# Passes that run there and back, two units' weights kept at each turn, and a DMA that adds the sums

## The chip, the core and the metric

The kernel runs on one core of a Trainium2 chip. The metric is the device time of one execution in microseconds (us). Every row below comes from one profiled execution of the kernel before; PE is TensorE, DVE VectorE, ACT ScalarE, POOL GpSimd, SP SyncE, whose queue issues nearly all transfers.

## The reference

```python
def reference(**kw):
    attn = _attn_ref(q, k, v)                 # 4 x 8 heads, 576 x 64: (scale * q k^T * decay mask) v
    x = attn.transpose(0, 2, 1, 3).reshape(2304, 512)
    h = np.maximum(x @ moe_w_in, 0.0)         # 512 -> 2048
    x = (h * h) @ moe_w_out                   # 2048 -> 512
    a, b = x @ moe2_w_a, x @ moe2_w_b         # 512 -> 1536 each
    return (a * b) @ moe2_w_out               # 1536 -> 512
```

The inputs of the MLPs come in float64 and are converted on the chip. All products need fp32 accuracy: each operand is split into a high and a low part of type fp32r, and each product is three matmuls (high by high, low by high, high by low).

## The kernel before, in words

**Stages.** The attention and four chunks of the first MLP (chunks 0 to 3 of 16, each 128 hidden columns) run first, over blocks of 512 tokens; their down sums go through `tmp` to `y1` in DRAM. Then `rest` does what is left in six **passes** of 768 tokens, two halves `j` of N2 = 384 columns each: phase 1 (`ph` 1) is chunks 4 to 15 of the first MLP, three passes; phase 2 is the twelve chunk pairs (a, b) of the second MLP, three passes.

**Units.** A pass is a list of units: six in phase 1 (two chunks each), twelve in phase 2. A unit is 2 x 2 blocks of products done with seven products instead of eight (`group`, banks 4 to 7 of PSUM): 42 matmuls of 384 columns. Its weights are two **pieces**, of 1024 and 768 columns, that were combined and stored in DRAM beforehand (`kept`). `piece(u)` loads both and splits them (`fetch`, `split`: an ACT CAST for the high part, a DVE subtraction for the low one, line 247 through the helper). There is room for the pieces of two units; unit u + 2 is loaded when unit u is done.

**Downs.** A finished hidden block goes down into banks 0 to 3, interleaved with the next units' products. A plain chunk costs 24 matmuls over both halves. Where `SEVENS` says so, pairs of chunks go down by seven products instead of eight (`sevens`): 42 matmuls for a pair in place of 48, for more combining of hidden blocks on DVE and ACT and more columns of combined weights. `put` adds a finished group of sums into `xt`, the SBUF tile that holds the 2304 tokens: at the end of phase 1 it holds the input of phase 2.

**First sums.** In phase 1 `x_prep` splits and combines the pass's tokens out of `xt` (tiles `xo` and `xb`), and then one DMA on SP loads what the first four chunks gave, `y1`, into the same columns of `xt`; every `put` of phase 1 then adds to it.

**Order.** Nothing is ordered by the loop's text alone: each step goes into a `Plan` with the engines that may run it, what it reads and writes, and its cost; `Plan.order` gives each step a latest time, counted back from PE's, and emits the steps engine by engine by that time. Float64 conversions (lines 369 to 399), which prepare later weights, have late due times and fill the gaps.

Line 238 is every matmul, 247 every subtraction, 250 every addition, 244 every copy or cast.

Of the kernel before, what the change touches and what calls it, by code (L numbers as in the profile page):

```python
# [17 lines left out]
ALU = mybir.AluOpType  # L18
# [4 lines left out]
P = 128  # L23
NP = H // 2
KT = DM // P
# [13 lines left out]
CHUNKS = {1: range(4, 16), 2: range(0, 12)}  # L39
N2 = 384  # L40
PASSES = NT // (2 * N2)
PIECES, OUTS = 8, 5
RUN, LAG = {1: 2, 2: 3}, {1: 1, 2: 2.5}
SEVENS = {(2, 0): [range(6, 12)], (2, 1): [range(0, 6), range(6, 12)], (2, 2): [range(0, 6), range(6, 12)], (1,1):[range(4,8)],(1,2):[range(4,8)]}
AFTER = 0.0
SPAN = 0.8
MORE = (2, 0, 6)
# [160 lines left out]
def act(n, psum=False):  # L208
    return 0.833 * n + (110 if psum else 140)

def dve(n):
    return 1.042 * n + 70
# [8 lines left out]
def tile_retention_two_mlps(  # L221
# [21 lines left out]
    def copy(o, i):  # L243
        return lambda e: A.copy(o(), i()) if e == "ACT" else eng[e].tensor_copy(o(), i())  # L244
# [4 lines left out]
    def add(o, a, b):  # L249
        return lambda e: eng[e].tensor_add(o(), a(), b())  # L250
# [4 lines left out]
    def dma(o, i):  # L255
        return lambda e: nc.sync.dma_start(out=o(), in_=i())

    def dmac(bytes_):
        return {"DMA": max(620.0, bytes_ / 310.0)}
# [61 lines left out]
    def tokens(name, k, c0, n):  # L321
        return [(name, k, j) for j in range(c0 // 32, (c0 + n) // 32)]
# [583 lines left out]
    def rest():  # L906
# [17 lines left out]
        for tag, size, wide in (("wp", WP, 2048), ("we", WE, 1024), ("late", RAWS, 2048)):  # L924
            for i in range(size):
                for j in range(wide // n):
# [2 lines left out]
                        return x.bitcast(F32)[:, n * j:n * j + n]  # L929

                    more.append((tile_, (f"{tag}{j}", i), (tag, i)))
        turn = {"piece": 0}
        gfree, tfree = list(gtiles), list(ttiles)
        ofree = list(range(PIECES, PIECES + OUTS))

# [5 lines left out]
        def x_prep(ph, p):  # L941

            c0 = 2 * n * p

            def blk(i, j):
                return lambda: xt[:, 2 * i:2 * i + 2, c0 + j * n:c0 + j * n + n]

            def kb(i, j):
                return [k for m in (2 * i, 2 * i + 1) for k in tokens("xt", m, c0 + j * n, n)]

            def halves_(o, i, j):
                for k in xkeys[o]:
                    plan.renew(k)
                hk, lk = [k + (0,) for k in xkeys[o]], [k + (1,) for k in xkeys[o]]
                plan.add(
                    {"ACT": act(2 * n)}, copy(lambda: xo[o][:, 0], blk(i, j)), kb(i, j), hk, [state_["entered"]]
                )
                plan.add(
                    {"DVE": dve(2 * n)}, sub(lambda: xo[o][:, 1], blk(i, j), lambda: xo[o][:, 0]),
                    kb(i, j) + hk, lk, [state_["entered"]],  # L960
                )

            def comb(to, x, y):
                plan.add({"DVE": dve(2 * n)}, sub(blk(*to), blk(*x), blk(*y)), kb(*x) + kb(*y), kb(*to))

            halves_(0, 0, 0)
            comb((0, 0), (0, 1), (0, 0))
            halves_(1, 0, 0)
            halves_(2, 1, 0)
            comb((0, 0), (1, 1), (0, 0))  # L970
            halves_(3, 0, 0)
            halves_(4, 1, 1)
            comb((0, 1), (1, 1), (0, 1))
            halves_(5, 0, 1)
            comb((1, 0), (1, 0), (0, 0))
            halves_(6, 1, 0)

            if ph == 1:
                plan.add(
                    dmac(P * 8 * n * KT), dma(lambda: xt[:, :, c0:c0 + 2 * n], lambda: y1[:, :, c0:c0 + 2 * n]),  # L980
                    [k for m in range(KT) for k in tokens("y1", m, c0, 2 * n)],
                    [k for m in range(KT) for k in tokens("xt", m, c0, 2 * n)],
                )

        units = [(ph, p, c) for ph in (1, 2) for p in range(PASSES) for c in CHUNKS[ph][::3 - ph]]
        at = {unit: u for u, unit in enumerate(units)}
        pieces = {}

        def piece(u):
            pass_["now"] = units[u][1]  # L990
            ph, _, c = units[u]
            for q, m in ((0, 1024), (1, 768)):
                i = 2 * (turn["piece"] % (PIECES // 2))
                turn["piece"] += 1
                pieces[units[u], q] = i
                plan.renew(("w", i))
                plan.renew(("w", i + 1))

                def to(i=i, m=m):
                    w = ws[i // 2]  # L1000
                    return w[:, 0, :m], w[:, 1, :m], w[:, :, :m]

                name = ph, q, c
                whole = slice(0, m)
                fetch(
                    to, [(whole, kept[ph, c, q], ("kept", (ph, c, q)))], m,
                    [("w", i, h) for h in range(2)], [("w", i + 1, h) for h in range(2)], name,
                )

        jobs = []  # L1010
        for ph in (1, 2):
            for p in range(PASSES):
                cs = list(CHUNKS[ph])
                sevens = SEVENS.get((ph, p), [])
                while cs:
                    run = next((list(r) for r in sevens if cs[0] in r), None)
                    if run:
                        k = at[ph, p, run[-1]] + 1 if ph == 2 else at[ph, p, run[-2]] + 1
                        jobs.append(("sevens", ph, p, run, len(run) * 21 / 12, k + AFTER, None, cs[0] == CHUNKS[ph][0]))
                        cs = cs[len(run):]  # L1020
                        continue
                    part = []
                    while cs and not any(cs[0] in r for r in sevens):
                        part.append(cs.pop(0))
                    seen, j, size = [0, 0], 0, RUN[ph]
                    fresh = part[0] == CHUNKS[ph][0]
                    k0 = at[ph, p, part[0] - (part[0] - CHUNKS[1][0]) % 2 if ph == 1 else part[0]] + LAG[ph]
                    k1 = k0 + len(part) / (2 if ph == 1 else 1)
                    rows = []
                    while min(seen) < len(part):  # L1030
                        a, b = seen[j], min(seen[j] + size, len(part))
                        rows += [(j, part[i], i == a, i == b - 1, fresh and a == 0) for i in range(a, b)]
                        seen[j], j, size = b, 1 - j, 2 * RUN[ph]
                    jobs.append(("plain", ph, p, rows, 2 * len(part), k0, k1, None))
# [162 lines left out]
        def put(ph, p, m, j, b, fresh, done):  # L1197

            c0 = (2 * p + j) * n
            d = lambda: xt[:, m, c0:c0 + n]  # L1200
            kd, a, ka = tokens("xt", m, c0, n), bank[b], ("bank", b)
            if ph == 2 and fresh:
                plan.add({"ACT": act(n, True), "DVE": dve(n)}, copy(d, lambda: a[:, :n]), [ka], kd)
            else:
                plan.add({"DVE": dve(n)}, add(d, lambda: a[:, :n], d), [ka], kd)
            if done:
                plan.add(dmac(P * 4 * n), dma(lambda: out[:, m, c0:c0 + n], d), kd)

        def plain(ph, p, j, c, start, last, fresh, done):
            gh, kgh = made.pop((ph, p, j, c))  # L1210
# [31 lines left out]
        def sevens(x, ph, p, run, fresh, done):  # L1242
# [44 lines left out]
            def side(o, u):  # L1287
                b, a = u, 2 + u
                kb, ka = ("bank", b), ("bank", a)
                pa = {"ACT": act(n, True)}  # L1290
                if o == 0:
                    plan.add(pa, copy(lambda: bank[a][:, :n], lambda: bank[b][:, :n]), [kb], [ka])
                elif o == 1:
                    put(ph, p, u, 0, b, fresh, done)
                elif o == 2:
                    put(ph, p, u, 1, b, fresh, False)
                    put(ph, p, 2 + u, 1, b, fresh, False)
                elif o == 3:
                    plan.add(pa, copy(lambda: bank[b][:, :n], lambda: bank[a][:, :n]), [ka], [kb])
                elif o == 4:  # L1300
                    put(ph, p, 2 + u, 1, b, False, done)
                elif o == 5:
                    put(ph, p, u, 1, a, False, done)
                else:
                    put(ph, p, 2 + u, 0, b, fresh, done)
# [26 lines left out]
        def lowers():  # L1332
            for x, job in enumerate(jobs):
                kind, ph, p, what = job[:4]
                end = ph == 2 and final[ph, p] == x
                if kind == "plain":
                    for j, c, start, last, fresh in what:
                        tail = end and last and c == what[-1][1]
                        yield from plain(ph, p, j, c, start, last, fresh, tail)
                else:  # L1340
                    yield from sevens(x, ph, p, what, job[7], end)
# [114 lines left out]
```

## Time and profile before

| | |
|---|---|
| median of 3 runs | 847.68 us (847.29 to 850.26) |
| the profiled execution's own time | 846.6 us |
| span of its instructions | 844.9 us |
| granted TensorE clock | 0.997 |
| PE, DVE, ACT, POOL busy | 826.7, 761.8, 595.7, 0.7 us |
| moved by DMA | 172.29 MB |

The span runs from the first to the last instruction; 1.7 us lie around it. A matmul counts as busy until its last result is out, so one of 384 columns shows 0.335 us although the next starts some 0.17 us after it.

### The profile page before, as it was taken

To read this page: it belongs to the slowest core of one execution; us is meant where nothing else is said; L and a number is where in the kernel's file an instruction comes from. 1 tells how busy PE (TensorE), PEld (TensorE's weight loads), DVE (VectorE), ACT (ScalarE), POOL (GpSimd) and SP (SyncE) were. 2 spreads that over 40 slices of the span, in tenths; PEclk is the share of its full clock that TensorE was granted. 3 is DMA by queue.
4 is the path that set the end of the run, shared out by engine and by line. 5 is a ranking of instruction groups with operands and counts; after the bars stand their busy time and mean duration, and the time that the engine had idled before them with its cause. 6 is when DMAs were issued, how large, how long until landed. Compare 5 with 4: busy or idle time off the path is not lost.

```text
span 844.9 us, 16923 instructions
## 1 busy us (share of the span) xinstructions
PE 826.7 (98%) x6540; PEld 801.8 (95%) x6540; DVE 761.8 (90%) x1269; ACT 595.7 (71%) x1067; POOL 0.7 (0%) x6
## 2 busy tenths in 40 slices
PE   6799999999999999999999999999999999999998
PEld 5688788999999999999999999999999999999997
DVE  7998889969999999999999999999886799897786
ACT  5785766778887978897895666576557586566553
POOL 0000000000000000000000000000000000000000
PEclk9999999999999999999999999999999999999999
DMA  8778976788867476573846798544543344544324
GB/s 310 287 236 280 304 257 200 263 304 275 291 214 238 136 235 232 181 258 121 285 159 225 262 299 259 182 136 148 151 156 121 123 136 139 169 142 139 106 68 133
DMA packets 68288, 172.29 MB, mean 204 GB/s; under 512 B 7280, under 2 KB 28016, under 8 KB 65392
## 3 DMA queue, kind: packets, MB, share of 16 engines
q1 hardware_dynamic: 68064, 171.21, 61.0%
q8 instruction: 51, 0.84, 0.4%
q14 instruction: 29, 0.24, 0.1%
q10 hardware_dynamic: 144, 0.01, 0.0%
HBM read 134.75 MB, written 36.44 MB: 203 GB/s over the span
## 4 chain that ended last, share of the span: by engine, by line
PE 95%; DMA 2%; DVE 2%; issue 1%; ACT 0%; DVEq 0%; ACTq 0%
PE bank L238 95%; DMA y<-tmp 1%; DMA w<-kept 0%; DMA vt<-vtab 0%; DVE sc L700 0%; ACT w L244 0%; DVE xt L667 0%; DVE pt L682 0%; DVE wp L399 0%; DVE wp L388 0%; DVE xb L247 0%; DVE wp L380 0%; DVE wp L373 0%; ACT ghl L1182 0%; DVE w L247 0%
## 5 line engine op out<-in xcount | busy, mean ns | idle before, releaser
L238 PE MATMUL bank<-xo,w 128*128 128x384 f32 x1946 | 406.2, 335 | 1.0 <-ACT bank L244 0.6
L238 PEld LDWEIGHTS bank<-xo,w 128*128 128x128 f32 x1946 | 343.3, 188 | 1.8 <-ACT bank L244 1.0
L238 PE MATMUL bank<-xb,w 128*128 128x384 f32 (+2 forms) x924 | 204.1, 346 | 3.0 <-ACT xb L244 1.8
L247 DVE TENSOR_TENSOR w<-w 128x512 fp32r<-128x512 f32 (+3 forms) x211 | 185.1, 885 | 14.1 <-ACT w L244 13.8
L244 ACT CAST w<-w 128x512 fp32r<-128x512 f32 (+3 forms) x211 | 161.4, 781 | 51.6 <-DMA w<-kept 50.3
L238 PEld LDWEIGHTS bank<-xb,w 128*128 128x128 f32 x924 | 163.6, 189 | 11.9 <-ACT xb L244 1.9
L238 PE MATMUL bank<-gh,w 128*128 128x384 f32 (+2 forms) x606 | 138.4, 350 | 0.0
L238 PEld LDWEIGHTS bank<-gh,w 128*128 128x128 f32 x606 | 106.6, 188 | 7.9 <-issue 0.4
L238 PE MATMUL bank<-w,w 128*128 128x384 f32 x486 | 109.4, 334 | 0.0
L244 ACT COPY bank<-bank 128x384 f32<-128x384 f32 x136 | 63.3, 467 | 46.4 <-PE bank L238 36.5
L238 PEld LDWEIGHTS bank<-w,w 128*128 128x128 f32 x486 | 86.5, 188 | 0.1
L238 PE MATMUL bank<-ghl,w 128*128 128x384 f32 x372 | 84.1, 335 | 0.4 <-DVE ghl L247 0.4
L250 DVE TENSOR_TENSOR xt<-bank,xt 128x384 f32<-128x384 f32 x140 | 75.9, 553 | 5.8 <-PE bank L238 4.2
L238 PEld LDWEIGHTS bank<-ghl,w 128*128 128x128 f32 x372 | 66.2, 188 | 1.1 <-DVE ghl L247 0.7
L399 DVE CUSTOM_DVE_ANT_0 wp<-wp,we 128x2048 uint16<-128x2048 uint16 (+1 forms) x35 | 41.6, 1189 | 0.2
L247 DVE TENSOR_TENSOR wp<-wp 128x256 f32<-128x256 f32 (+1 forms) x82 | 34.2, 426 | 0.2
L247 DVE TENSOR_TENSOR xo<-xt,xo 128x768 fp32r<-128x768 f32 x36 | 33.6, 953 | 0.0
L395 ACT ACTIVATE we<-raw 128x1024 int32<-128x1024 uint32 x24 | 27.6, 1150 | 5.5 <-DVE wp L399 5.2
L244 ACT CAST xo<-xt 128x768 fp32r<-128x768 f32 x36 | 29.2, 836 | 1.0 <-PE bank L238 0.6
L388 DVE SCALAR_TENSOR_TENSOR wp<-raw,wp 128x1024 uint32<-128x1024 uint32 x24 | 29.2, 1219 | 0.0
L369 ACT ACTIVATE wp<-raw 128x1024 f32<-128x1024 f32 x24 | 27.4, 1141 | 1.9 <-DMA kept<-wp 1.9
L373 DVE TENSOR_SCALAR wp<-wp 128x1024 f32<-128x1024 f32 (+1 forms) x35 | 23.6, 674 | 5.0 <-ACT wp L369 4.9
(246 smaller groups left out, 941.6 us busy)
## 6 DMA issues: line engine op xcount, KB each, us to landing
w<-kept SPq DMA_DIRECT2D x54, 512.0 KB, 3.6
raw<-w SPq DMA_DIRECT2D x24, 1024.0 KB, 6.0
w<-kept SPq DMA_DIRECT2D x54, 384.0 KB, 3.4
w<-kept SPq DMA_DIRECT2D x133, 128.0 KB, 3.0
kept<-wp SPq DMA_DIRECT2D x22, 512.0 KB, 4.1
w<-kept SPq DMA_DIRECT2D x34, 256.0 KB, 3.5
wraw<-w SPq DMA_DIRECT2D x8, 1024.0 KB, 7.3
kept<-wp SPq DMA_DIRECT2D x8, 1024.0 KB, 6.0
```

Source lines behind the costliest of these rows:

```text
L238: T.matmul(o, l, r, start=start, stop=stop, skip_group_check=True)
L244: return lambda e: A.copy(o(), i()) if e == "ACT" else eng[e].tensor_copy(o(), i())
L247: return lambda e: eng[e].tensor_sub(o(), a(), b())
L250: return lambda e: eng[e].tensor_add(o(), a(), b())
L369: {"ACT": act(n)}, lambda e: A.activation(like(w()), hi().bitcast(F32), AF.Abs), [kraw], kw
L373: lambda e: V.tensor_scalar(out=w(), in0=w(), scalar1=F64_MIN, scalar2=F64_MAX, op0=ALU.max, op1=ALU.min),
L388: lambda e: V.scalar_tensor_tensor(out=like(wu()), in0=hi(), scalar=0xC0000000, in1=like(wu()), op0=ALU.bitwise_and, op1=ALU.bitwise_or),
L395: lambda e: A.activation(like(rest[:, :n]), lo(), AF.Copy, scale=LO_ULPS), [kraw], [ke],
L399: lambda e: V._custom_dve(ADD32_U16LIMBS, out=w().bitcast(U16), in0=w().bitcast(U16), in1=rest[:, :n].bitcast(U16)),
```

## The change

Three edits. The passes of each phase run through their units forward, backward, forward, and at a turn the two units whose pieces are still in SBUF use them again (`piece` returns early: nothing is loaded or split). In phase 1 `y1` is no longer loaded ahead: the first group of sums is copied into `xt`, and after the last group one DMA for each 128 x 384 block, issued from POOL with an adding write, adds `y1`. And `SEVENS` in phase 1 covers six pairs (chunks 8 to 11 in pass 1, 4 to 11 in pass 2) in place of four (4 to 7 in both). Beside them, the two puts of a sevens run that take the same bank become one instruction over 2 x 384 columns (`put_two`).

```diff
-SEVENS = {..., (1,1):[range(4,8)],(1,2):[range(4,8)]}
+SEVENS = {..., (1,1):[range(8,12)],(1,2):[range(4,8),range(8,12)]}
...
-            if ph == 1:
-                plan.add(
-                    dmac(P * 8 * n * KT), dma(lambda: xt[:, :, c0:c0 + 2 * n], lambda: y1[:, :, c0:c0 + 2 * n]),
...
+        order = {
+            (ph, p): list(CHUNKS[ph])[::1 - 2 * (p % 2)] for ph in (1, 2) for p in range(PASSES)
+        }
...
         def piece(u):
             pass_["now"] = units[u][1]
             ph, _, c = units[u]
+            back = next((d for d in (1, 3) if u >= d and units[u - d][::2] == units[u][::2] != units[u - 2][::2]), None)
+            if back:
+                for q in range(2):
+                    pieces[units[u], q] = pieces[units[u - back], q]
+                return
             for q, m in ((0, 1024), (1, 768)):
-                i = 2 * (turn["piece"] % (PIECES // 2))
-                turn["piece"] += 1
+                i = pieces[units[u - 2], q] if u > 1 else 4 * u + 2 * q
...
-            if ph == 2 and fresh:
+            if fresh:
                 plan.add({"ACT": act(n, True), "DVE": dve(n)}, copy(d, lambda: a[:, :n]), [ka], kd)
             else:
                 plan.add({"DVE": dve(n)}, add(d, lambda: a[:, :n], d), [ka], kd)
-            if done:
+            if done and ph == 2:
                 plan.add(dmac(P * 4 * n), dma(lambda: out[:, m, c0:c0 + n], d), kd)
+            elif done:
+                plan.add(
+                    dmac(P * 8 * n),
+                    lambda e: G.dma_start(out=d(), in_=y1[:, m, c0:c0 + n], accum_op=ALU.add),
+                    tokens("y1", m, c0, n), kd,
+                )
+
+        def put_two(ph, p, u, j, b, fresh):
+            c0 = (2 * p + j) * n
+            d, kd = lambda: xt[:, u::2, c0:c0 + n], [k for m in (u, 2 + u) for k in tokens("xt", m, c0, n)]
+            a, ka = lambda: bank[b][:, :n].unsqueeze(1).to_broadcast([P, 2, n]), ("bank", b)
+            if fresh:
+                plan.add({"ACT": act(2 * n, True), "DVE": dve(2 * n)}, copy(d, a), [ka], kd)
+            else:
+                plan.add({"DVE": dve(2 * n)}, add(d, a, d), [ka], kd)
```

How the instructions stand now is shown at three places. The first is PE where phase 1 begins: `gh_83,w_87` is the last of the first four chunks going down, `xo_1957,w_84` the first unit's first product. Before:

```order
L238 MATMUL bank_68<-gh_82,w_86 128x256
L238 MATMUL bank_71<-xo_1957,w_84 128x384
L238 MATMUL bank_72<-xo_1957,w_84 128x384
L238 MATMUL bank_70<-xo_1957,w_84 128x384 x6
L238 MATMUL bank_69<-xo_1958,w_84 128x384 x3
L238 MATMUL bank_65<-gh_83,w_87 128x256 x3
L238 MATMUL bank_66<-gh_83,w_87 128x256 x3
L238 MATMUL bank_67<-gh_83,w_87 128x256 x3
L238 MATMUL bank_68<-gh_83,w_87 128x256 x3
```

And with the change:

```order
L238 MATMUL bank_68<-gh_82,w_86 128x256
L238 MATMUL bank_65<-gh_83,w_87 128x256 x3
L238 MATMUL bank_66<-gh_83,w_87 128x256 x3
L238 MATMUL bank_67<-gh_83,w_87 128x256 x3
L238 MATMUL bank_68<-gh_83,w_87 128x256 x3
L238 MATMUL bank_71<-xo_1957,w_84 128x384
L238 MATMUL bank_72<-xo_1957,w_84 128x384
L238 MATMUL bank_70<-xo_1957,w_84 128x384 x6
```

The last downs now stand ahead of the first unit, where eleven of its matmuls stood before them.

The second is DVE at the same point: `w_84` to `w_87` are the low parts of the first two units' pieces, `wp` lines combine or convert later weights, `gh_83` is the low part that the last downs wait for. Before:

```order
L247 TENSOR_TENSOR w_1967<-w_1967 128x512
L247 TENSOR_TENSOR w_84<-w_84 128x1024
L247 TENSOR_TENSOR xb_76<-xt,xb_76 128x768
L247 TENSOR_TENSOR gh_83<-g_79,gh_83 128x256
L247 TENSOR_TENSOR wp_73<-wp_73 128x256
L399 ISA wp_74<-wp_74,we_75 128x2048
L244 COPY tmp_1969<-bank_65 128x256
L244 COPY tmp_1971<-bank_67 128x256
L247 TENSOR_TENSOR w_85<-w_85 128x768
```

And with the change:

```order
L250 TENSOR_TENSOR wp_73<-wp_73 128x256
L247 TENSOR_TENSOR wp_73<-wp_73 128x256 x3
L247 TENSOR_TENSOR gh_82<-g_78,gh_82 128x256
L247 TENSOR_TENSOR xb_76<-xt,xb_76 128x768
L247 TENSOR_TENSOR gh_83<-g_79,gh_83 128x256
L373 TENSOR_SCALAR wp_74<-wp_74 128x1024
L244 COPY tmp_1969<-bank_65 128x256
L247 TENSOR_TENSOR w_84<-w_84 128x1024
L247 TENSOR_TENSOR w_85<-w_85 128x768
```

The low part of `w_84` moved behind `gh_83`, and the conversion in front of it is four combinations further, since chunks 8 and 10 are now stored in the wide form that sevens read.

The third is SP's queue at the first turn, from pass 0 to pass 1 of phase 1; `kept_4_0` is the larger piece of chunk 4, `kept_4_4` its down weights. Before:

```order
L256 DMA w_1965<-kept_14_4_144 128x512
L256 DMA w_84<-kept_4_0_127 128x1024
L256 DMA kept_0_0_145<-wp_73 128x1024
L256 DMA w_1965<-kept_14_4_144 128x512
L256 DMA raw_1964<-w 128x2048
L256 DMA w_85<-kept_4_1_128 128x768
L256 DMA w_1966<-kept_4_4_129 128x256
L256 DMA kept_0_1_146<-wp_73 128x768
L256 DMA kept_1_0_147<-wp_74 128x1024
L256 DMA w_1966<-kept_6_4_132 128x256
L256 DMA w_86<-kept_6_0_130 128x1024
```

And with the change:

```order
L256 DMA w_1965<-kept_14_4_144 128x512 x2
L256 DMA kept_0_0_145<-wp_73 128x1024
L256 DMA raw_1964<-w 128x2048
L256 DMA w_1966<-kept_14_4_144 128x512
L256 DMA kept_0_1_146<-wp_73 128x768
L256 DMA w_1966<-kept_14_4_144 128x512
L256 DMA w_1967<-kept_12_4_141 128x512
L256 DMA kept_1_0_147<-wp_74 128x1024
L256 DMA w_86<-kept_10_0_136 128x1024
```

No pieces are loaded between the last units of pass 0 (chunks 12 and 14) and those of chunk 10; before, four loads stood there.

## Rows read from the trace of the kernel before

**Rows 1.** The page: busy time by engine, and the chain that ended last.
```profile
PE 826.7 (98%) x6540; PEld 801.8 (95%) x6540; DVE 761.8 (90%) x1269; ACT 595.7 (71%) x1067; POOL 0.7 (0%) x6
PE 95%; DMA 2%; DVE 2%; issue 1%; ACT 0%; DVEq 0%; ACTq 0%
```

**Rows 2.** Windows: stretch, its us, then PE, PEld, DVE, ACT, POOL, clock, DMA.
```profile
163.70:179.60 15.90, 14.48 (x84) 13.45 (x83) 10.44 (x17) 12.40 (x25) 0.00 (x0) 1.00 0.93 325
200.00:829.70 629.70, 629.70 (x3633) 629.38 (x3631) 581.47 (x979) 449.49 (x815) 0.00 (x0) 1.00 0.57 185
163.70:440.00 276.30, 274.88 (x1585) 273.84 (x1585) 264.02 (x438) 231.07 (x423) 0.00 (x0) 1.00 0.68 229
829.70:845.00 15.30, 11.78 (x66) 11.21 (x65) 8.96 (x17) 4.46 (x10) 0.00 (x0) 0.95 0.36 122
```

**Rows 3.** PE groups, 179.6 to 829.7 us: count, busy, mean ns, idle ahead.
```profile
L238 PE MATMUL bank<-xo,w 128*128 128x384 f32 x1896 | 395.9, 334 | 0.0
L238 PE MATMUL bank<-ghl,w 128*128 128x384 f32 x353 | 79.5, 335 | 0.4 <-DVE ghl L247 0.4
```

**Rows 4.** PE groups, 163.7 to 179.6 us, all of them.
```profile
L238 PE MATMUL bank<-xo,w 128*128 128x384 f32 x50 | 10.4, 343 | 1.0 <-ACT bank L244 0.6 <-DVE w L247 0.4
L238 PE MATMUL bank<-gh,w 128*128 128x384 f32 x12 | 2.6, 334 | 0.0
L238 PE MATMUL bank<-gh,w 128*128 128x256 f32 x13 | 1.9, 282 | 0.0
L238 PE MATMUL bank<-xb,w 128*128 128x384 f32 x6 | 1.2, 334 | 0.0
L238 PE MATMUL bank<-ghl,w 128*128 128x384 f32 x3 | 1.0, 372 | 0.4 <-DVE ghl L247 0.4
```

**Rows 5.** Timeline where phase 1 begins: start, us, engine, instruction, idle ahead.
```profile
161.07 1.15 ACT L395 ACTIVATE we<-raw 128x1024 int32<-128x1024 uint32 x1
...
162.56 1.05 ACT L244 CAST w<-w 128x1024 fp32r<-128x1024 f32 x1 [0.33 <-DMA w<-kept]
...
163.51 0.37 ACT L824 ACTIVATE r<-bank 128x256 f32<-128x256 f32 x1
...
166.42 1.59 PE L238 MATMUL bank<-gh,w 128*128 128x256 f32 x12
...
167.84 2.77 PE L238 MATMUL bank<-xo,w 128*128 128x384 f32 x15
...
178.10 0.96 DVE L247 TENSOR_TENSOR w<-w 128x768 fp32r<-128x768 f32 x1 [3.88 <-ACT w L244]
```

**Rows 6.** Groups by shape over the whole span: count, busy, mean ns, idle ahead.
```profile
L250 DVE TENSOR_TENSOR xt<-bank,xt 128x384 f32<-128x384 f32 x140 | 75.9, 553 | 5.8 <-PE bank L238 4.2
L247 DVE TENSOR_TENSOR w<-w 128x1024 fp32r<-128x1024 f32 x54 | 65.9, 1220 | 1.2 <-ACT w L244 1.0
L247 DVE TENSOR_TENSOR w<-w 128x768 fp32r<-128x768 f32 x54 | 51.5, 954 | 12.1 <-ACT w L244 12.1
L247 DVE TENSOR_TENSOR wp<-wp 128x256 f32<-128x256 f32 x78 | 32.0, 420 | 0.2
L244 ACT CAST w<-w 128x1024 fp32r<-128x1024 f32 x54 | 56.7, 1049 | 36.4 <-DMA w<-kept 36.4
L244 ACT CAST w<-w 128x768 fp32r<-128x768 f32 x54 | 45.2, 837 | 6.2 <-DMA w<-kept 6.1
L244 ACT COPY bank<-bank 128x384 f32<-128x384 f32 x136 | 63.3, 467 | 46.4 <-PE bank L238 36.5 <-DVE wp L253 4.7 <-DVE more L253 3.8
```

**Rows 7.** DVE lines 373 and 380, POOL's longest group, DMA issues: KB, us to landing.
```profile
L373 DVE TENSOR_SCALAR wp<-wp x35: 422/689/696, 14.0 to 522.2; 128x1024 f32<-128x1024 f32 x33, 128x512 f32<-128x512 f32 x2
L521 POOL TENSOR_SCALAR_AFFINE_SELECT mask<-mask 64x64 f32<-64x64 f32 x2 | 0.5, 235 | 3.0 <-DVE first L319 3.0
out<-xt SPq DMA_DIRECT2D x24, 192.0 KB, 1.9
xt<-y SPq DMA_DIRECT2D x3, 1536.0 KB, 6.9
```

More of the change, by code (lines that the diff above doesn't have):

```diff
@@ L43 @@
 RUN, LAG = {1: 2, 2: 3}, {1: 1, 2: 2.5}
-SEVENS = {(2, 0): [range(6, 12)], (2, 1): [range(0, 6), range(6, 12)], (2, 2): [range(0, 6), range(6, 12)], (1,1):[range(4,8)],(1,2):[range(4,8)]}
+SEVENS = {(2, 0): [range(6, 12)], (2, 1): [range(0, 6), range(6, 12)], (2, 2): [range(0, 6), range(6, 12)], (1,1):[range(8,12)],(1,2):[range(4,8),range(8,12)]}
 AFTER = 0.0
@@ L931, in rest @@
                     more.append((tile_, (f"{tag}{j}", i), (tag, i)))
-        turn = {"piece": 0}
         gfree, tfree = list(gtiles), list(ttiles)
@@ L976, in x_prep @@
             halves_(6, 1, 0)
-            if ph == 1:
-                plan.add(
-                    dmac(P * 8 * n * KT), dma(lambda: xt[:, :, c0:c0 + 2 * n], lambda: y1[:, :, c0:c0 + 2 * n]),
[L981 to L985, printed above, removed]
+        order = {
+            (ph, p): list(CHUNKS[ph])[::1 - 2 * (p % 2)] for ph in (1, 2) for p in range(PASSES)
+        }
+        units = [
+            (ph, p, c) for ph in (1, 2) for p in range(PASSES)
+            for c in order[ph, p] if ph == 2 or c % 2 == CHUNKS[1][0] % 2
+        ]
         at = {unit: u for u, unit in enumerate(units)}
@@ L1012, in rest @@
             for p in range(PASSES):
-                cs = list(CHUNKS[ph])
+                cs = list(order[ph, p])
+                begin = cs[0]
                 sevens = SEVENS.get((ph, p), [])
                 while cs:
-                    run = next((list(r) for r in sevens if cs[0] in r), None)
+                    run = next((list(r)[::2] for r in sevens if cs[0] in r), None)
                     if run:
-                        k = at[ph, p, run[-1]] + 1 if ph == 2 else at[ph, p, run[-2]] + 1
-                        jobs.append(("sevens", ph, p, run, len(run) * 21 / 12, k + AFTER, None, cs[0] == CHUNKS[ph][0]))
+                        run = [c + i for c in run[::1 - 2 * (p % 2)] for i in range(2)]
+                        k = max(at[ph, p, c] for c in run if (ph, p, c) in at) + 1
+                        jobs.append(("sevens", ph, p, run, len(run) * 21 / 12, k + AFTER, None, cs[0] == begin))
                         cs = cs[len(run):]
@@ L1025, in rest @@
                     seen, j, size = [0, 0], 0, RUN[ph]
-                    fresh = part[0] == CHUNKS[ph][0]
+                    fresh = part[0] == begin
                     k0 = at[ph, p, part[0] - (part[0] - CHUNKS[1][0]) % 2 if ph == 1 else part[0]] + LAG[ph]
@@ L1295, in side @@
                 elif o == 2:
-                    put(ph, p, u, 1, b, fresh, False)
-                    put(ph, p, 2 + u, 1, b, fresh, False)
+                    put_two(ph, p, u, 1, b, fresh)
                 elif o == 3:
@@ L1334, in lowers @@
                 kind, ph, p, what = job[:4]
-                end = ph == 2 and final[ph, p] == x
+                end = final[ph, p] == x
                 if kind == "plain":
```

## The prediction

> **What bounds the kernel now.** I read the page first: PE is busy 98% of the span, and the chain that ended last is PE for 95% of it [rows 1]. That share is an average, so the windows come next, and they split the span in two. From 200 to 829.7 us PE has 3633 matmuls in 629.7 us, 0.1733 us each, with every slice full [rows 2]. The groups of that stretch say the same from the other side: the idle time ahead of 1896 matmuls of units is 0.0, and the only wait of 0.4 us is the one at its very start [rows 3]. No later wait shows, though DVE is busy 264.0 of 276.3 us in phase 1 [rows 2]: its conversions are not urgent and give way. So from 180 us to the end the time is the number of matmuls, and what DVE, ACT or DMA save there is worth nothing by itself.
>
> The exception is where phase 1 begins, 163.7 to 179.6 us. It holds 71 matmuls of 384 columns and 13 of 256 [rows 4]. Twelve of the short ones take 167.84 - 166.42 = 1.42 us [rows 5], 0.118 each. The work is 71 x 0.1733 + 13 x 0.118 = 13.8 us in 15.9: about 2.1 us are lost. The page's own idle column names three waits of 0.4, 0.6 and 0.4 us: for the split of a piece, for a copy between banks and for the low part of a hidden block [rows 4].
>
> The sum below is made against the profiled execution, 846.6 us; the median shown is 847.68, 1.1 us more. I carry the difference of the two kernels over to the median.
>
> **The change, part by part.**
>
> *Sevens.* Four pairs become six. Each pair saves 48 - 42 = 6 matmuls, so 12 leave PE, which the order confirms: the unit products stay, and only 384-column downs go. 12 x 0.1733 = **-2.08 us**, taken in the saturated stretch.
>
> What they cost elsewhere: a pair needs three more splits of hidden blocks and four more differences (0.55 us each by the 384-column row), and chunks 8 and 10 are stored wide, eight combinations of 256 columns at 0.42 [rows 6], 3.4 us of DVE, all of it between 152 us and the end of the first units.
>
> *Kept units.* Two turns in each of two phases, two units, two pieces: eight splits of 1024 and eight of 768 columns go. On DVE 8 x (1.220 + 0.954) = 17.4 us, on ACT 8 x (1.049 + 0.837) = 15.1 us [rows 6], and 16 loads leave SP's queue. PE waits for none of them after 180 us [rows 3], so this is worth 0 on the path. A reused unit waits for nothing new: its data stand in SBUF, and the next unit's load is issued when the unit before has freed the place, one unit ahead as now.
>
> *First sums.* 3 loads of 1.5 MB leave SP, and 24 adding DMAs of 192 KB go to POOL. Nothing but `x_prep` of phase 2 reads the result: for the first two passes more than a pass later, and the last pass's sums end early in phase 2, with two passes of phase 2 still ahead of their reader. POOL's queue holds nothing else. So 0 on the path. The trace shows no adding DMA; one of the same size lands in 1.9 us, and the 1.5 MB load in 6.9 [rows 7]. Even 24 x 6.9 = 166 us one after the other would be spread over three passes, 92 us of PE each: still hidden.
>
> *Merged puts and copies.* 36 additions of 384 columns go (19.9 us at 0.553), ten double ones come (about 0.95 each, as a 768-column split). With the further splits, combinations and copies I add DVE up to 10 us less than before, and ACT to 3 us more (nine bank copies at 0.467 and 14 casts against the 15.1 us saved). Off the path: 0. The cover is DVE's idle 12 us in phase 1; without it each microsecond would count.
>
> *Where phase 1 begins.* Here the order itself changes, and DVE's 3.4 us come at the worst place. Bounds: all 2.1 us lost there come back (-2.1), or the eight combinations all stand in PE's way (+3.4). Following the new order with the old durations: ACT used to run a conversion (1.15) and a cast (1.05) just ahead of the last ReLU, at 163.51 [rows 5]; now the token cast alone stands there, and the ReLU starts some 0.8 us earlier. The low part `gh_83` then ends near 164.4, PE waits about 0.7 us for it, and its twelve downs end at 165.8. ACT has a conversion and the cast of `w_84` behind that ReLU, until 166.1, and DVE's low part another 1.2 us: PE waits 0.3 and 0.9. That is 1.9 us of new waits in place of about 1.0 in the first half. In the second half the old loss goes: the split of `w_87` came late, at 178.10, after 3.9 us of DVE waiting for ACT [rows 5]; it now stands six microseconds earlier, ahead of what PE needs. I get to the same point of PE's program, the low part of the second unit's first hidden block, 0.2 to 0.6 us sooner. I take **-0.3 us**.
>
> *The end.* The last 66 matmuls take 11.4 of 11.8 us, and DVE's last addition and one store follow [rows 2]; the last run of sevens keeps its shape. 0.
>
> Sum: -2.08 - 0.3 = -2.4 us: 844.2 for an execution like the profiled one, **845.3 us** against the median.
>
> **A rule that speaks against it.** Line 373 passes 1024 columns in 0.689 us, where a subtraction takes 1.220 [rows 6, 7], so DVE has a fast mode there, and it runs until 522 us, beyond the last DMA of phase 1. The Trainium skill (SBUF — State Buffer, section SBUF: two separate sides) says that such an operation and POOL share one pair of ports under an exclusive lock: a DMA issued from POOL can't have its descriptors written meanwhile, and whichever starts first blocks the other whole. By its first half the adding DMAs are late, which costs nothing here. By its second half DVE would wait for POOL; no row before shows it, since POOL works 0.7 us in all [rows 1]. As a mechanism of this kernel it is the first rival below.
>
> **The rivals.**
>
> *POOL holds DVE up (slower).* Place: the ends of the three passes of phase 1. Price: 24 times x. Below, x is 0 or POOL's longest operation, 0.235; above, the whole landing of such a store, 1.9 [rows 7]. DVE has 12.3 us of idle and saves about 7 in phase 1, so it decides only from x = 19.3 / 24 = 0.8 us. At the middle, 1.07, it is 25.7 - 19.3 = +6.4: 851.7; at 1.9 it is +26: 871. For it: DVE is nearly full there. Against: only the fast operations can collide. 0.06.
>
> *First sums wait for `x_prep` (slower).* The first copies into `xt` must come after all 11 DVE operations of `x_prep` (0.95 each, 10.5 us) where the load used to bear that wait. If banks 0 to 3 stood full meanwhile, up to 10 us in each of three passes: 855 with a third of it. Against: the first unit's hidden blocks aren't ready for the first downs before those reads are over; PE's seven products are themselves the readers' users. 0.06.
>
> *The matmuls are saved and given back (no change).* Sevens copy banks on ACT four times in a run (0.467 each, 1.9 us), and PE must not overtake them. One run more, with two in a row in pass 2: -2.4 + 1.9 = 847.2. Against: of seven such runs none cost PE anything visible [rows 3]. 0.10.
>
> *The start of phase 1 clears altogether.* -2.08 - 2.1 = -4.2: 843.5. For it: 1.5 MB less on a DMA that is 0.93 busy there [rows 2]. 0.12.
>
> **How the numbers follow.** My forecast holds 0.66, with its own range 844.3 to 846.3. Half a per cent is about what a measurement of this kernel can tell from no change: 4.2 us, so faster means below 843.4 and slower above 851.9. The forecast, the rival that gives the matmuls back and a sixth of the last lie between: 0.78 for same. Faster is the rest of the last rival, 0.10; slower is the first two, 0.12. The range of 843.2 to 849.0 leaves out most of those two and the best of the fast end.
>
> **What would show it.** Right: 3872 matmuls of 384 columns at 0.173, a stretch from 200 us to the last downs without idle time, 1.5 to 2.5 us lost between 163.7 and 180, DVE's busy time some 10 us lower, POOL's DMAs in three groups of eight. Wrong: PE waits at the ends of the passes of phase 1 with fast DVE operations stretched beyond 0.69 us (POOL), idle time in front of downs at their starts (first sums), or PE waiting for ACT's bank copies in a run of sevens.

## The result and the profile after

| | before | after |
|---|---|---|
| median of 7 runs | 847.29 us (845.2 to 850.26) | 853.31 us (850.94 to 856.3) |
| the profiled execution, its span | 846.6, 844.9 us | 853.31, 851.6 us |
| matmuls of 384 columns | 3884 | 3872 |
| DVE, ACT, POOL busy | 761.8, 595.7, 0.7 us | 755.5, 593.9, 22.0 us |
| moved by DMA | 172.29 MB | 166.78 MB |

The ratio is 1.007 (95% interval 1.0044 to 1.0096): the change costs 6 us. Less work is done on PE, DVE, ACT and DMA, and the kernel is slower.

The page of the kernel after: busy times, the two DMA queues (packets, MB, share of 16 engines' span), the chain that ended last, and the new DMA group with its idle time.

```profile
PE 828.8 (97%) x6528; PEld 803.2 (94%) x6528; DVE 755.5 (89%) x1258; ACT 593.9 (70%) x1076; POOL 22.0 (3%) x30
q1 hardware_dynamic: 65616, 160.98, 57.0%
q0 software_dynamic: 3456, 4.72, 3.6%
PE 90%; DMA 4%; DVE 3%; ACT 2%; issue 1%; SPq 0%; DVEq 0%; ACTq 0%
L1215 POOL DMA_DIRECT2D xt<-y x24 | 21.4, 919 | 439.1 <-DVE xt L250 265.3 <-DVE wp L380 76.6 <-ACT w L244 70.4
```

Against [rows 1], PE holds 90% of the chain in place of 95%, and DMA twice as much. Where that happens is seen by counting matmuls. In a saturated stretch one takes 0.1733 us, so those missing from a stretch, against the same stretch of before, are time lost there. Windows of the kernel after (stretch, its us, then PE, PEld, DVE, ACT, POOL, clock, DMA share, GB/s):

```profile
255.00:285.00 30.00, 28.73 (x166) 28.41 (x165) 23.72 (x41) 20.16 (x38) 7.35 (x8) 1.00 0.80 202
285.00:345.00 60.00, 60.00 (x346) 59.57 (x345) 58.80 (x102) 51.65 (x100) 0.00 (x0) 1.00 0.58 182
345.00:380.00 35.00, 33.24 (x183) 32.92 (x182) 31.50 (x56) 26.31 (x51) 7.00 (x8) 0.95 0.79 214
435.00:480.00 45.00, 43.83 (x251) 43.19 (x251) 42.38 (x70) 29.98 (x53) 7.02 (x8) 1.00 0.78 227
480.00:575.00 95.00, 95.00 (x550) 94.98 (x549) 93.47 (x154) 62.24 (x104) 0.00 (x0) 1.00 0.69 235
```

The same stretches of the kernel before:

```profile
255.00:285.00 30.00, 30.00 (x175) 30.00 (x174) 29.61 (x52) 23.62 (x49) 0.00 (x0) 1.00 0.60 206
...
345.00:380.00 35.00, 35.00 (x204) 34.99 (x203) 34.67 (x65) 29.81 (x60) 0.00 (x0) 1.00 0.71 241
435.00:480.00 45.00, 45.00 (x262) 45.00 (x261) 44.75 (x74) 29.40 (x50) 0.00 (x0) 1.00 0.58 194
480.00:575.00 95.00, 95.00 (x550) 95.00 (x549) 91.75 (x150) 64.39 (x108) 0.00 (x0) 1.00 0.70 227
```

From 285 to 345 us it held 348. So 9, 2, 21, 11 and 0 are missing: 1.6 + 0.3 + 3.6 + 1.9 = 7.5 us. The three stretches that lose are the ends of the three passes of phase 1, and they are the three in which POOL works: its eight DMAs each stand there.

That accounts for the profiled difference of 6.7 us: -2.1 (twelve matmuls), -1.0 (where phase 1 begins: from the run of twelve token products of 256 columns, which starts at 157.07 us and before at 155.00, to the first matmul that reads the low part of a `ghl` block it takes 23.54 us, 24.58 before), +7.5 at the three turns, 0.3 not placed, and +2.1 in the first 155 us. The last is no effect of the change: the instructions there are the same, and in the ten profiles of the experiments below the start of those twelve lies anywhere from 153.3 to 158.2 us.

At the second turn the chain that ended last reads so (start, us, what):

```profile
339.87 22.74 PE bank L238 x132
362.61 6.34 DMA w<-kept
...
368.97 0.83 ACT w L244
369.80 0.39 ACT bank L244
...
370.23 14.84 PE bank L238 x75
```

And its timeline (start, us, engine, instruction, idle time before it and what ended that):

```profile
367.55 0.88 POOL L1215 DMA_DIRECT2D xt<-y  x1 [3.37 <-ACT gh L244]
...
368.97 0.83 ACT L244 CAST w<-w 128x768 fp32r<-128x768 f32 x1 [2.34 <-DMA w<-kept]
...
369.71 0.47 ACT L244 COPY bank<-bank 128x384 f32<-128x384 f32 x1
...
370.23 3.87 PE L238 MATMUL bank<-xo,w 128*128 128x384 f32 x12 [1.76 <-ACT bank L244]
```

Read from the bottom: PE waits 1.76 us for a copy between banks. The copy takes 0.47 and waits for no data; it stands on ACT behind the cast of a piece, and the cast waits 2.34 us for its load. The page's idle column would name the bank copy; the chain names the load.

The loads are late because of what runs beside them. DMA issues from 345 to 380 us after (queue, count, KB each, median us to landing), with the queues' share of 16 engines:

```profile
q1 hardware_dynamic: 2306, 5.92, 50.2%
q0 software_dynamic: 1129, 1.54, 28.5%
...
xt<-y POOLq DMA_DIRECT2D x8, 192.0 KB, 7.0
w<-kept SPq DMA_DIRECT2D x9, 128.0 KB, 6.5
...
w<-kept SPq DMA_DIRECT2D x2, 512.0 KB, 7.0
...
kept<-wp SPq DMA_DIRECT2D x1, 512.0 KB, 8.3
```

And before, where the same stretch holds the 1.5 MB load of `y1`:

```profile
q1 hardware_dynamic: 3536, 8.39, 70.4%
...
w<-kept SPq DMA_DIRECT2D x3, 512.0 KB, 4.8
w<-kept SPq DMA_DIRECT2D x10, 128.0 KB, 3.3
```

The 128 KB loads land in 6.5 us in place of 3.3. The load that PE waits for is one of 384 KB; it lands in 6.34, and in 3.7 where the adding DMAs are left out (e6 below). The medians of that size don't show this: the two such loads of this stretch take 4.9 us, and 5.6 before, where PE waited for neither. Fewer bytes move (7.5 MB against 8.4), but they occupy the engines longer: 28.5% of 16 x 35 us is 160 engine-us for 1540 KB of adding writes, 104 ns per KB, where the rest costs 281 / 5920 KB = 47 after and 394 / 8390 KB = 47 before.

What is not the cause: DVE's fast operations. Line 373 of the kernel after (least/median/most ns, first to last start):

```profile
L373 DVE TENSOR_SCALAR wp<-wp x35: 419/686/696, 13.2 to 538.8; 128x1024 f32<-128x1024 f32 x33, 128x512 f32<-128x512 f32 x2
```

The longest is 0.696 us, as before [rows 7]. Two fast operations, of lines 380 and 373, started while POOL was issuing a DMA, at 260.82 and 361.92 us; they took 0.689 and 0.683. So no fast operation is seen to be held by POOL.

### The profile page after: what moved, and what is told of

It reads as the page before. It is cut to its first block, busy times and chain, and to the rows that moved or that the text cites. A ratio compares the mean times of both kernels' runs of the same rounds, so it can differ in the third digit from the quotient of the medians.

```text
span 851.6 us, 16947 instructions
## 1 busy us (share of the span) xinstructions
PE 828.8 (97%) x6528; PEld 803.2 (94%) x6528; DVE 755.5 (89%) x1258; ACT 593.9 (70%) x1076; POOL 22.0 (3%) x30
## 2 busy tenths in 40 slices
DMA packets 69296, 166.78 MB, mean 196 GB/s; under 512 B 7520, under 2 KB 33120, under 8 KB 66144
## 3 DMA queue, kind: packets, MB, share of 16 engines
q0 software_dynamic: 3456, 4.72, 3.6%
## 4 chain that ended last, share of the span: by engine, by line
PE 90%; DMA 4%; DVE 3%; ACT 2%; issue 1%; SPq 0%; DVEq 0%; ACTq 0%
PE bank L238 90%; DMA w<-kept 2%; DVE w L247 1%; DMA vr<-vk 1%; DMA kept<-wp 1%; DMA vt<-vtab 0%; DVE xo L247 0%; DVE xt L250 0%; ACT w L244 0%; ACT tv L594 0%; ACT wp L369 0%; DVE xt L247 0%; DVE xt L667 0%; DVE xb L247 0%; ACT bank L244 0%
## 5 line engine op out<-in xcount | busy, mean ns | idle before, releaser
L247 DVE TENSOR_TENSOR w<-w 128x512 fp32r<-128x512 f32 (+3 forms) x198 | 170.1, 865 | 21.4 <-ACT w L244 20.6
L244 ACT CAST w<-w 128x512 fp32r<-128x512 f32 (+3 forms) x198 | 149.0, 765 | 49.5 <-DMA w<-kept 49.3
L244 ACT COPY bank<-bank 128x384 f32<-128x384 f32 x140 | 65.5, 468 | 49.9 <-PE bank L238 37.9
L250 DVE TENSOR_TENSOR xt<-bank,xt 128x384 f32<-128x384 f32 (+1 forms) x114 | 66.3, 588 | 5.9 <-PE bank L238 4.9
L1215 POOL DMA_DIRECT2D xt<-y x24 | 21.4, 919 | 439.1 <-DVE xt L250 265.3
```

Source lines behind the costliest of these rows:

```text
L247: return lambda e: eng[e].tensor_sub(o(), a(), b())
L1215: lambda e: G.dma_start(out=d(), in_=y1[:, m, c0:c0 + n], accum_op=ALU.add),
```

## The experiments

Each ratio is against the kernel before on the same chip, with its 95% interval. In the expectations A is the theory that the adding DMAs hold PE up at the turns, B that the passes there and back do, C that the extra sevens do. D came up after the first four: more work on DVE in phase 1 makes the float64 conversions late, and PE waits behind them, around 540 us. "Missing" is always the count of 384-column matmuls against before in the same stretch, times 0.1733.

**e1: no adding DMA; `y1` loaded ahead as before, the rest of the change kept.**

```diff
+            if ph == 1:
+                plan.add(... dma(lambda: xt[:, :, c0:c0 + 2 * n], lambda: y1[:, :, c0:c0 + 2 * n]), ...)
-            if fresh:
+            if ph == 2 and fresh:
...
-            elif done:
-                plan.add(... G.dma_start(out=d(), in_=y1[:, m, c0:c0 + n], accum_op=ALU.add), ...)
```

> The changed kernel with its first-sums part alone undone: y1 is loaded ahead on SP and every put of phase 1 adds. Theory A (the adding DMAs take the DMA engines from the weight loads at the ends of the phase 1 passes, each lands in 7.0 us, and PE waits there): the waits of the turns go and the 12 saved matmuls show, ratio to before 0.995 to 0.999 (843 to 846 us). Rival B (the turns themselves, forward and backward with kept pieces, bunch the loads): still 1.004 to 1.009. Rival C (the sevens in the middle of a pass and two in a row make PE wait): still 1.003 or more.

Measured 852.48 us, ratio 1.0063 (1.0047 to 1.008). The waits of the second and third turn go, 1.4 us stay at the first, and a new loss appears where the kernel after has none:

```profile
480.00:575.00 95.00, 90.75 (x510) 87.69 (x510) 92.69 (x152) 61.40 (x100) 0.00 (x0) 1.00 0.71 241
```

40 of 550 matmuls are missing, 6.9 us. The ratio lies where B and C had it, so A by itself does not explain the slowdown.

**e2: the kernel before with copied first sums and the 24 adding DMAs alone.**

```diff
-            if ph == 1:
-                plan.add(... load of y1 into xt ...)
-            if ph == 2 and fresh:
+            if fresh:
...
-            if done:
+            if done and ph == 2:
...
+            elif done:
+                plan.add(... G.dma_start(out=d(), in_=y1[:, m, c0:c0 + n], accum_op=ALU.add), ...)
```

> The kernel before with the first-sums part alone: first group copied, y1 added by 24 DMAs from POOL. Theory A: 1.004 to 1.010 (851 to 856 us), PE waits at the ends of the three passes of phase 1, landings of about 7 us. Rivals B and C: 0.999 to 1.002.

Measured 856.37 us, ratio 1.0118 (1.0097 to 1.0139). Its windows at the turns:

```profile
255.00:285.00 30.00, 29.06 (x167) 28.62 (x166) 28.57 (x50) 22.75 (x47) 7.15 (x8) 1.00 0.81 201
345.00:380.00 35.00, 33.29 (x192) 32.78 (x191) 31.73 (x57) 27.52 (x58) 7.02 (x8) 1.00 0.81 234
435.00:480.00 45.00, 42.57 (x235) 41.93 (x234) 40.45 (x67) 27.11 (x47) 7.35 (x8) 0.96 0.67 184
```

8, 12 and 27 matmuls are missing, 8.2 us, and none later (the profiled execution took 853.25 us, 3.1 below the median; the ratio is somewhat above what A allowed). This part alone makes the waits of the change, at the places of its DMAs.

**e3: the kernel before with six pairs of sevens in phase 1 in place of four.**

```diff
-..., (1,1):[range(4,8)],(1,2):[range(4,8)]}
+..., (1,1):[range(8,12)],(1,2):[range(4,8),range(8,12)]}
```

> The kernel before with the six pairs alone. Theory A: 12 x 0.1733 = 2.1 us less, ratio 0.996 to 0.999. Rival C: 1.002 or more, with PE waits at the runs of sevens of phase 1. Rival B: as theory A.

Measured 860.08 us, ratio 1.0152 (1.013 to 1.0174): twelve matmuls less, and the slowest of all. DVE's busy time is 775.3 us, 13.5 more than before. The window that loses, and DVE's timeline in it:

```profile
480.00:575.00 95.00, 84.04 (x451) 80.61 (x450) 90.56 (x152) 57.32 (x89) 0.00 (x0) 0.95 0.79 262
```

```profile
536.33 1.22 DVE L388 SCALAR_TENSOR_TENSOR wp<-raw,wp 128x1024 uint32<-128x1024 uint32 x1
537.46 0.69 DVE L373 TENSOR_SCALAR wp<-wp 128x1024 f32<-128x1024 f32 x1
538.07 1.22 DVE L399 CUSTOM_DVE_ANT_0 wp<-wp,we 128x2048 uint16<-128x2048 uint16 x1
539.20 0.69 DVE L380 TENSOR_SCALAR wp<-wp 128x1024 uint32<-128x1024 uint32 x1
...
544.09 1.22 DVE L247 TENSOR_TENSOR w<-w 128x1024 fp32r<-128x1024 f32 x1
...
545.36 2.93 PE L238 MATMUL bank<-xo,w 128*128 128x384 f32 x8 [7.39 <-DVE w L247]
```

99 matmuls are missing, 17 us. The sevens cost nothing where they run; DVE falls behind in phase 1, and 100 us later its queue holds conversions ahead of the split of a piece. PE waits 7.39 us for that split, which itself takes 1.22. The size is beyond both theories, and the place is neither's: this is where D came from.

**e4: the passes there and back with kept pieces alone** (e1 with four pairs of sevens and the double puts apart again).

```diff
-..., (1,1):[range(8,12)],(1,2):[range(4,8),range(8,12)]}
+..., (1,1):[range(4,8)],(1,2):[range(4,8)]}
...
-                    put_two(ph, p, u, 1, b, fresh)
+                    put(ph, p, u, 1, b, fresh, False)
+                    put(ph, p, 2 + u, 1, b, fresh, False)
```

> The kernel before with the passes there and back and the kept pieces alone (y1 loaded ahead, four pairs, two puts apart). Theory A: no work leaves PE, 0.999 to 1.001. Rival B: 1.004 or more, PE waits at the turns. Rival C: as theory A.

Measured 846.88 us, ratio 0.9998 (0.9984 to 1.0011). No wait of PE after 200 us; DVE does 13.0 us less, and line 399, the last operation of a conversion, shows it: its last start is 519.7 us, against 527.8 before and 552.6 in e3 (rows of e4 and e3).

```profile
L399 DVE CUSTOM_DVE_ANT_0 wp<-wp,we x35: 682/1217/1226, 16.7 to 519.7; 128x2048 uint16<-128x2048 uint16 x33, 128x1024 uint16<-128x1024 uint16 x2
```

```profile
L399 DVE CUSTOM_DVE_ANT_0 wp<-wp,we x35: 681/1218/1226, 16.6 to 552.6; 128x2048 uint16<-128x2048 uint16 x33, 128x1024 uint16<-128x1024 uint16 x2
```

B is out: nothing is lost at the turns. The kept units are worth nothing by themselves, and what they free on DVE is what the sevens then spend.

**e5: the change with plain writes in place of adding ones** (`y1` then overwrites the sums of phase 1 instead of being added).

```diff
-                    lambda e: G.dma_start(out=d(), in_=y1[:, m, c0:c0 + n], accum_op=ALU.add),
+                    lambda e: G.dma_start(out=d(), in_=y1[:, m, c0:c0 + n]),
```

> The changed kernel with the 24 DMAs of POOL as plain writes: y1 overwrites the sums, so that part of the result is left out. Theory A1 (it is the adding write that is dear: 104 ns of a DMA engine for each KB against 48 on SP's queue): each lands in 3 to 4 us, most of the waits at the three turns go, 0.997 to 1.001. Theory A2 (it is POOL's queue or the extra 4.7 MB at the turns, whatever the DMA does): still 1.004 to 1.009 and landings of 6 us or more.

Measured 850.56 us, ratio 1.0043 (1.0027 to 1.0059). The queue moves the same bytes for half the engine time:

```profile
q0 software_dynamic: 1536, 4.72, 1.8%
```

1.8% of 16 x 848.8 us for 4.72 MB is 52 ns per KB. The first turn no longer loses anything, the third 1.2 us; the second still loses 4.2. Part of the cost is the adding, part the bytes at that place; how much of each is not settled by this run: the ratio lies in the range of the second theory, the landings, 5.3 us in the median, between the two. The queue's packets are fewer too, 1536 in place of 3456 for the same bytes, so what is called the adding here may be the smaller packets. At the second turn PE waits 1.52 us for a cast, behind a load that lands in 7.79, and from 370 to 375 us the granted clock is 0.74; so part of the 4.2 is the clock.

**e6: the change with the adding DMAs left out** (`y1` is missing from the sums).

```diff
-            elif done:
-                plan.add(... G.dma_start(out=d(), in_=y1[:, m, c0:c0 + n], accum_op=ALU.add), ...)
```

> The changed kernel with the 24 adding DMAs left out, so that y1 is missing from the result. Theory A (they alone make the changed kernel slow; copied first sums and kept units pay VectorE for the two more pairs of sevens): no PE wait after 180 us, 0.995 to 0.999 (843 to 847 us). Rival C (sevens cost PE by their own chain of bank copies): 1.003 or more.

Measured 848.22 us, ratio 1.0012 (0.9998 to 1.0025). No wait is left at the turns, but the gain expected is not there either:

```profile
480.00:575.00 95.00, 93.03 (x523) 91.71 (x522) 87.73 (x146) 58.53 (x97) 0.00 (x0) 0.98 0.62 210
```

27 matmuls are missing there, 4.7 us, which takes back the 3.1 us gained before. The profiled execution took 851.55 us, 3.3 above the median; by the ratio (+1.0 us) and the 3.1 gained the loss is some 4.1. The last start of line 399 is 540.2 us. From 345 to 380 us the 128 KB loads land in 3.5 us, as before the change (3.3), and not in 6.5: that shows the adding DMAs as what makes them late. So the change has a second loss, which the waits at the turns hide: they give DVE time.

**e7: the adding DMAs kept, but spread over a later pass** (the last eight over pass 1 of phase 2). Each waits for a one-element POOL copy that reads a hidden block of a later unit.

```diff
+        def add_late(unit):
+            ...
+            plan.add({"POOL": 200}, look, rd, [("gate", 0)])
+            _, d, y, ky, kd = pending.pop(0)
+            plan.add(dmac(P * 8 * n), lambda e: G.dma_start(out=d(), in_=y(), accum_op=ALU.add), ky + [("gate", 0)], kd)
...
-                plan.add(... G.dma_start(out=d(), in_=y1[:, m, c0:c0 + n], accum_op=ALU.add), ...)
+                pending.append((p, d, lambda: y1[:, m, c0:c0 + n], tokens("y1", m, c0, n), kd))
...
+            if (ph == 1 and p and u % 6 > 1) or (ph, p) == (2, 1):
+                for _ in range(2 if ph == 1 else 1):
+                    if pending:
+                        add_late(unit)
```

> The changed kernel with the adding DMAs taken away from the turns: each waits, by a copy of one element on POOL, for a hidden block of a later unit: two behind each of the last four units of passes 1 and 2 of phase 1, and one behind each of eight units of pass 1 of phase 2. Theory A with the place as cause (they meet the loads at the turns): 0.995 to 1.000. With their amount as cause, wherever they stand: 1.003 to 1.009.

Measured 850.74 us, ratio 1.0038 (1.0024 to 1.0053).

```profile
285.00:345.00 60.00, 58.53 (x336) 57.89 (x336) 57.09 (x97) 50.06 (x97) 12.97 (x16) 1.00 0.68 199
480.00:575.00 95.00, 92.26 (x526) 90.65 (x525) 90.93 (x149) 59.80 (x98) 1.20 (x2) 1.00 0.66 225
```

The turns lose next to nothing (2 matmuls at the third), the stretch behind the first 2.1 us, and the conversions' stretch 4.2. The ratio lies where it was expected if only the amount counted, but the windows divide it: the same 24 transfers cost 2 us in place of 7.5, so place matters. The 4.2 us are lost where e6, without any of them, loses 4.7, and are put down to D.

**e8: the kernel before, with 24 subtractions of 384 columns repeated on DVE** in passes 1 and 2 of phase 1 (24 x 0.553 = 13.3 us by the length of their records).

```diff
+            if name[0] == 1 and name[1] > 0 and name[3] % 4 != 3:
+                plan.add({"DVE": dve(n)}, sub(lambda: gh()[:, 1], g, lambda: gh()[:, 0]), [kg, kgh + (0,)], [kgh + (1,)])
```

> The kernel before with 24 subtractions of 384 columns on DVE done twice in passes 1 and 2 of phase 1, 13.3 us more DVE, about what two more pairs of sevens add. Theory D (DVE's conversions are a budget that is spent to the last by 575 us, and sevens alone lost by it): 10 to 14 us more, 1.010 to 1.017, with the PE waits between 480 and 575 us. Rival C: below 1.003.

Measured 856.75 us, ratio 1.011 (1.0091 to 1.0128).

```profile
480.00:575.00 95.00, 89.77 (x503) 89.13 (x502) 90.84 (x147) 62.33 (x101) 0.00 (x0) 0.96 0.73 245
```

47 matmuls are missing, 8.1 us, in the same stretch, without any change to sevens or transfers. DVE's busy time, where records that overlap count once, is 770.4 us: 8.6 more than before, against the 13.5 of e3. The chain that ended last (start, us, what) is DVE's own work up to a copy between banks, for which PE waits 5.20 us:

```profile
540.27 1.14 DVE wp L399
541.41 0.48 DVE wp L250
...
541.91 0.47 ACT bank L244
...
542.43 2.61 PE bank L238 x7
```

The copy on ACT waits for the addition of line 250, and that stands on DVE behind a conversion. D holds.

**e9: e1 with five pairs of sevens.**

```diff
-..., (1,1):[range(8,12)],(1,2):[range(4,8),range(8,12)]}
+..., (1,1):[range(4,8)],(1,2):[range(4,8),range(8,10)]}
```

> A version that may beat both: passes there and back with kept pieces and merged puts, y1 loaded ahead on SP (no adding DMA), and five pairs by sevens (chunks 4 to 7 in pass 1, 4 to 9 in pass 2) in place of six. Theory D (the conversions' deadline): kept units ended the last conversion 8 us earlier in their own run (519.7 against 527.8 us), and one more pair costs DVE some 6.5 us, so it just fits: no PE wait after 181 us, six matmuls less, 0.997 to 1.000. If the budget is already spent: PE waits between 480 and 575 us and 1.001 to 1.005.

Measured 850.53 us, ratio 1.0031 (1.0016 to 1.0046): 535 matmuls in the stretch, 2.6 us lost, between e1's 6.9 (six pairs) and e4's nothing (four). DVE had already no room for a fifth pair, though its busy time in the whole span, 753.8 us, is 8.0 below that of before: what counts is the work ahead of the last conversions, and two of the four turns, which save DVE work, lie behind them.

**e10: e6 with four pairs of sevens** (`y1` is missing here too).

```diff
-..., (1,1):[range(8,12)],(1,2):[range(4,8),range(8,12)]}
+..., (1,1):[range(4,8)],(1,2):[range(4,8)]}
```

> The changed kernel with the adding DMAs left out (y1 missing from the result) and four pairs as before. Theory D: the 4.7 us that PE lost between 480 and 575 us with six pairs are gone, the last conversion starts before 528 us, no PE wait after 181 us, 0.997 to 1.000. If something other than the two more pairs made those waits (the copied first sums, the turns): they stay, 1.002 to 1.005.

Measured 847.35 us, ratio 0.9992 (0.9979 to 1.0006).

```profile
480.00:575.00 95.00, 95.00 (x550) 95.00 (x549) 84.92 (x142) 58.31 (x102) 0.00 (x0) 1.00 0.50 169
```

DVE has 10 us of idle time there, and nothing is missing. With both causes away nothing is lost, and nothing is gained.

The three edits can be read off these runs. There and back: 0.9998 (e4). Six pairs instead of four, with no transfer of `y1`: 0.9992 becomes 1.0012 (e10, e6), +1.7 us, with intervals that overlap. The adding DMAs, with six pairs: 1.0012 becomes 1.007 (e6, after), +4.9 us. These steps are no fixed prices: with `y1` loaded ahead six pairs cost 5.5 us against four (e4, e1, where the double puts come along), and in the kernel before 12.9 (e3). No version tried is faster than before by what can be measured.

## Why the prediction was wrong

Predicted 845.3, measured 853.3, above the range. By its own steps:

- **Twelve matmuls, -2.08.** Right: 3872 are left, at 0.1733. They buy nothing, as the points on first sums and conversions show.
- **Where phase 1 begins, -0.3.** The sign was right, the size small: 1.0 us came back.
- **First sums, "so 0 on the path".** This is the step that failed. It asked who reads the result of the 24 DMAs and when, and found them in time, even if each took 6.9 us; they take 7.0 and are in time. It did not ask what else the DMA engines do while they run. `put` of the last group is also where the next pass's pieces are loaded, and ACT holds the bank copies that PE needs behind the casts of those loads. In place of 0 the runs show 4.9 us (after against e6), and 8.2 us of waits when nothing else is changed (e2).
- **Its price.** The nearest row was a plain store of 192 KB in 1.9 us [rows 7]. In the change the adding writes land in 7.0, at 104 ns per KB of engine time against 47 for the transfers beside them. The 1.5 MB load that they replace cost its bytes once, at 47. The Trainium skill (DMA: Bandwidth & Descriptors, section Rules for kernel authors) says that an accumulating DMA reads its destination and writes it later. The trace does not show the reading; it shows more engine time for each byte, 104 against 52 for the same bytes written plainly (e5).
- **"Its conversions are not urgent and give way".** The second step that failed. DVE runs its instructions in the order written by `Plan.order`; a conversion gives way when the order is made, and not when the engine is late. The prediction put DVE's cover at 12 us idle in phase 1 and took any sum below that as free. e8 shows that 24 more subtractions, 8.6 us of DVE's busy time, cost PE 8.1 us; e3, that the sevens alone, priced at some 11 us, cost 13.5 of DVE and 17 of PE. In the change the turns' 7.5 us of waits hide this, so the two losses don't add up; without the DMAs 4.7 us of it appear (e6).
- **Kept units, 0; merged puts, 0.** Kept units: right by themselves (e4). DVE came out 6.3 us lower, where up to 10 was expected. The merged puts were not run alone.
- **The rivals.** "POOL holds DVE up" named the right three places and a price, +6.4 us, close to what came, for a wrong reason. The Trainium skill (SBUF — State Buffer, section SBUF: two separate sides) would let POOL's descriptor writing block a fast DVE operation whole; no such operation is longer than 0.697 us, those that started during an issue of POOL included, so the trace does not show it. First sums waiting for `x_prep`: not seen. Matmuls given back by bank copies in a run of sevens: not there; e3 gives them back eight times over, through DVE. The start that clears altogether: half of it came.

What stays open: how the cost at a turn divides between the adding itself, its smaller packets and the bytes (e5), and why the second turn loses as much with plain writes (4.2 us) as with adding ones (3.6), beyond the fall of the clock that both show. Also open is why e1 still loses 1.4 us at the first turn, about what the change loses there (1.6): PE's longest wait is for the same operation, the square on ACT that makes a hidden block, 1.24 us in e1 and 1.27 after, so the loss at that turn can't be put down to the adding writes alone. A third buffer for conversions, and combinations on POOL instead of DVE, which could relieve DVE, were not tried.

## What to carry to other kernels

A transfer that nobody waits for soon is still paid for by the loads that share its engines: price it in engine time, and look for the queue in which an urgent instruction stands behind one of those loads. Idle time of an engine that runs in order is no free cover for work added earlier; find the last time at which its background work must be done, and how far that already slides. Before stacking edits, run each alone: here one loss hid another, and taking the adding DMAs back (e1) brought next to nothing.

## What was not expected of the hardware

- The adding DMA writes (DRAM to SBUF, f32) take 104 ns per KB of engine time, in 3456 packets; the same bytes written plainly 52, in 1536 (e5).
- A POOL issue of one takes 0.919 us in the mean, of a plain one 0.578 (e5).
- A wait can cost more than itself. After the 1.76 us wait at 368.5 the granted clock is 0.58 over 4 us; within these it is 0.50 from 371 to 374 us, the lower of its two levels (1.2 GHz, and 2.4 at 1.00), after PE had stood still where it had run at 1.00. Windows of the kernel after around it:

```profile
366.00:370.00 4.00, 2.47 (x15) 2.15 (x13) 1.78 (x5) 1.61 (x4) 1.35 (x2) 1.00 1.02 266
370.00:374.00 4.00, 3.77 (x13) 3.77 (x14) 3.51 (x7) 3.38 (x8) 1.25 (x2) 0.58 1.09 337
374.00:378.00 4.00, 4.00 (x25) 4.00 (x24) 3.97 (x6) 3.23 (x9) 0.87 (x1) 0.99 1.07 239
```

13 matmuls in 4 us, where 23 fit at 1.00; the first 0.23 us still belong to the wait, so about 1.5 of the 3.6 us lost at this turn are the clock. At the other two turns, where the longest waits were 1.27 and 0.83 us, it stayed at 1.00. The length of the wait alone does not tell: after 1.66 us in e6 the clock was 0.66 from 540 to 545 us, after 1.71 us at the second turn of e2 it stayed at 1.00.
